# Moving forty-eight hand-over markers and output copies between VectorE, SyncE and ScalarE in a hand-ordered attention and MoE kernel

## The chip, the cores and the metric

The kernel runs on one core of one Trainium2 chip. The metric is device time in microseconds (us) for one launch. Before the change the median of three runs is 328.45 us (328.18 to 328.79).

The engines are TensorE (PE, its weight loads shown apart as PEld), VectorE (DVE), ScalarE (ACT), GpSimd (POOL) and SyncE (SP). Each has its own queue of instructions. Here SyncE computes nothing: it issues DMAs and carries markers that only wait and signal.

## The reference

Softcapped attention over 8 batches of 12 heads, 448 positions, 64 wide, followed by a block with two input matrices and an elementwise maximum:

```python
scores = cap * tanh(scale * q @ k.T / cap)
attn = exp(scores - max) / sum(exp(scores - max))
x = (attn @ v), heads joined to rows of 768
out = maximum(x @ w1, x @ w2) @ w_out      # 768 -> 1024 -> 768
```

## The kernel before, in words

**Tiling and stages.** The heads are taken in 48 pairs (`i`) and 24 quads of heads (`t`). Of a pair, `S i j` computes a block of scores on TensorE (L522), `T` and `E` run tanh and exp on ScalarE (L527, L544), `A` and `B` add up exponentials on VectorE (L556, L561), `VL` and `V` multiply by the values on TensorE (L608, L614), and `N` normalizes on VectorE into `xT` (L626, L629). From quad 5 on the queries and keys of a quad are turned by a DMA transpose that SyncE issues (`cr t`, line 483, `qkT<-kqs`). `qkT` has two buffers, so the transpose for quad `t` must wait until the last scores of quad `t-2` have read theirs.

The block behind the attention is rewritten as relu(x(w1-w2)) w_out + x(w2 w_out). It is cut into 120 groups, and each group accumulates in one PSUM bank: `stage1` groups make 128 columns of `gT` for one batch (448 columns stream per matmul, operands `xT` and `wd_sb`), `stage2` groups make 128 rows by 384 columns of output (operands `xT`, `wm_sb` for six steps, then `gT`, `wo_sb` for eight). Every two batches have 30 groups.

**Two half matmuls at a time.** A step of 128 contraction rows is split into two matmuls of 64 rows, one on each half of TensorE's rows. `M x y n` issues `n` times a first-half matmul of group `x` on the one row half and a second-half matmul of group `y` on the other (lines 640 to 656; all of these stand at L653 in the profile). A group does all its steps of one half, then all of the other half. While a group changes from one row half to the other, the first matmul of the new half must not start before the last one of the old half has left the PSUM bank.

**The hand-over.** `Group.hand_over(eng)` (line 660) writes a marker, an instruction that does nothing, into the queue of engine `eng` (L662). The marker waits for the group's last matmul of the old half; the group's first matmul of the new half waits for the marker (line 655). `H g` puts it on VectorE, `Hs g` on SyncE. An engine runs its queue in the order of the program, so a marker also waits for what stands ahead of it there, and holds up what stands behind it.

**The order.** The whole program is one string, `ORDER` (from line 10), executed literally under a manual schedule. No planner changes it. Apart from `S`, `M` and so on, SyncE's queue gets `cr` (transposes), `st b t` (two output stores each, L684, L685, L689) and the `Hs` markers. VectorE's queue gets the `H` markers between its sums, normalizations, the relu of stage 1 (L674) and `ev g`, which copies a finished stage-2 bank to the output buffer (L710). `eva g` does that copy on ScalarE (L708). POOL issues the loads.

Places that the later parts speak of, in the order string of before: `cr 11`, `H 29` and `H 28` (lines 78, 79 and 80), `cr 16`, `H 55` (line 119), `Hs 70` (line 146), `st 6 1` with `H 102`, and `st 6 2` with `H 105` (line 198).

Of the kernel before, what the change touches and what calls it, by code (L numbers as in the profile page):

```python
# [70 lines left out]
T 18 0; M 26 25 2; H 24; M 26 25 1; M 24 25 1; lk 23 1; M 24 25 1; E 17 0 2; H 26; M 24 25 1; S 18 2; M 24 25 1;  # L71
lq 23 0; M 24 25 4; S 18 1; O 27 3; M 27 25 1; eva 24; M 27 25 1; A 8 1 1; M 27 25 1; M 27 26 1; T 18 1;
M 27 26 2; ev 25; M 27 26 3; B 8 0; T 18 2; M 27 26 1; st 1 4; M 27 26 3; A 8 0 2; M 27 26 1; Hs 27; E 17 2 3;
O 28 1; M 28 26 2; B 8 1; L 9; st 0 2; VL 8; TL 9; V 8 0 0 2; A 8 1 2; V 8 1 0 2; E 18 0 3; Y 8 2; V 8 0 2 3;
V 8 1 2 3; Y1 8; lk 24 0; S 19 0; M 28 26 1; M 28 27 1; Y2 8; M 28 27 1; lv 10 0; Hs 26; st 1 3; M 28 27 1;
Y3 8; M 26 27 3; lv 10 1; M 26 27 1; N 8 0; M 26 27 2; T 19 0; lv 10 2; M 26 27 1; Hs 28; M 26 27 1; N 8 1;
O 29 2; M 29 27 2; lv 10 3; EL 9; M 29 27 1; M 29 28 1; S 19 1; M 29 28 1; lk 24 1; M 29 28 2; T 19 1; ev 26;
S 19 2; M 29 28 1; ev 27; M 29 28 1; lq 24 0; cr 11; M 29 28 1; T 19 2; M 29 28 1; A 9 0 1; S 20 0; M 29 28 2;
lk 25 0; M 29 28 1; E 19 0 2; A 9 0 2; O 30 3; M 30 28 1; S 20 1; M 30 28 1; H 29; lk 25 1; M 30 28 1;
M 30 29 2; H 28; st 1 5; M 30 29 1; lq 25 0; M 28 29 2; T 20 0; M 28 29 1; A 9 1 1; M 28 29 4; T 20 1; B 9 0;  # L80
Hs 30; M 28 29 1; S 20 2; O 31 0; M 31 29 1; B 9 1; M 31 29 1; eva 28; M 31 29 1; M 31 30 2; T 20 2; ev 29;
M 31 30 1; O 32 1; M 32 30 2; H 31; st 1 6; M 32 30 1; E 19 2 3; L 10; ev 30; VL 9; V 9 0 0 2; TL 10; A 9 1 2;
V 9 1 0 2; M 32 31 1; E 20 0 3; Y 9 3; V 9 0 2 3; V 9 1 2 3; lk 26 0; Y1 9; S 21 0; M 32 31 2; Y2 9; lv 11 0;
O 33 3; M 33 31 1; Y3 9; M 33 31 1; Hs 32; M 33 31 1; lv 11 1; M 33 32 2; N 9 0; T 21 0; M 33 32 1; O 34 2;
M 34 32 1; lv 11 2; M 34 32 1; Hs 33; ev 31; M 34 32 1; EL 10; lv 11 3; S 21 1; N 9 1; M 34 33 3; lk 26 1;
T 21 1; O 35 0; M 35 33 2; Hs 34; M 35 33 1; M 35 34 1; lq 26 0; ev 32; S 21 2; S 22 0; M 35 34 1; T 21 2;
ev 33; M 35 34 1; lk 27 0; O 36 1; M 36 34 2; A 10 0 1; Hs 35; M 36 34 1; E 21 0 2; M 36 35 1; lk 27 1; S 22 1;
ev 34; M 36 35 2; O 37 3; M 37 35 1; A 10 0 2; lq 27 0; M 37 35 1; Hs 36; M 37 35 1; M 37 36 1; T 22 0;
M 37 36 1; ev 35; M 37 36 1; O 38 2; M 38 36 2; A 10 1 1; Hs 37; cr 12; M 38 36 1; T 22 1; M 38 37 1; S 22 2;
B 10 0; M 38 37 2; T 22 2; O 39 0; M 39 37 1; ev 36; M 39 37 2; E 21 2 3; H 38; B 10 1; M 39 38 3; ev 37; L 11;  # L90
VL 10; TL 11; A 10 1 2; V 10 0 0 2; V 10 1 0 2; E 22 0 3; Y 10 1; V 10 0 2 3; V 10 1 2 3; Y1 10; S 23 0;
M 39 38 2; Y2 10; M 39 38 2; Y3 10; M 39 38 4; N 10 0; O 40 3; M 40 38 2; T 23 0; Hs 39; M 40 38 1; M 40 39 1;
N 10 1; M 40 39 1; Hs 38; M 40 39 1; EL 11; M 38 39 2; lk 28 0; S 23 1; M 38 39 3; T 23 1; A 11 0 1; lv 12 0;
S 23 2; M 38 39 2; cr 13; A 11 0 2; M 38 39 1; lv 12 1; T 23 2; O 41 1; M 41 39 1; S 24 0; ev 38; M 41 39 2;
lv 12 2; M 41 40 1; E 23 0 2; M 41 40 1; ev 39; S 24 1; M 41 40 1; lv 12 3; M 41 40 3; lk 28 1; M 41 40 1;
st 2 0; M 41 40 3; T 24 0; M 41 40 1; A 11 1 1; lq 28 0; O 42 2; M 42 40 3; H 41; T 24 1; B 11 0; M 42 41 1;
S 24 2; Hs 40; lk 29 0; M 42 41 2; B 11 1; M 40 41 1; T 24 2; M 40 41 1; lk 29 1; M 40 41 4; E 23 2 3;
M 40 41 1; lq 29 0; M 40 41 1; O 43 0; M 43 41 1; ev 40; L 12; VL 11; A 11 1 2; TL 12; V 11 0 0 2; V 11 1 0 2;
E 24 0 3; Y 11 3; V 11 0 2 3; V 11 1 2 3; Y1 11; S 25 0; M 43 41 2; Y2 11; M 43 42 2; Y3 11; M 43 42 4; N 11 0;
# [687 lines left out]
```

## Time and profile before

| what | value |
|---|---|
| median of 3 runs | 328.45 us |
| the profiled execution | 328.8 us |
| its span, first to last instruction | 327.0 us |
| granted TensorE clock | 0.997 |
| instructions in the span | 9770 |

A profile shows one execution. Its span is 1.8 us shorter than that execution's own time, which in turn lies 0.35 us above the median of the three runs. Groups of instructions are named by line, engine and tiles, `out<-in`. "SPq" and "DVEq" are instructions that only the engine's sequencer handles (markers, DMA issues); they do not count as busy time. A matmul's record (323 ns for 384 columns, 349 ns for 448) is longer than the distance at which matmuls of one row half follow each other, because they are pipelined, so the PE's busy share says little about small holes.

### The profile page before, as it was taken

What the parts mean: (1) busy time and instruction counts of PE and PEld (TensorE: products, weight loads), DVE (VectorE), ACT (ScalarE), POOL (GpSimd) and SP (SyncE); (2) the same over time, 40 slices, a digit from 0 to 9 for tenths busy, and PEclk for the clock granted to TensorE, in tenths of its full rate; (3) what the DMA queues carried; (4) which work ended last, traced back from release to release, by engine and by line L of the source; (5) the groups of instructions that cost most, each with busy time, mean ns of one, the idle gap of its engine ahead of it and who ended that gap; (6) DMA issues with size and microseconds to landing.
All of it is one profiled execution on the core that took longest, in us unless ns stands there. A gap on an engine that the chain in (4) does not pass through costs nothing.

```text
span 327.0 us, 9770 instructions
## 1 busy us (share of the span) xinstructions
PE 319.7 (98%) x4136; PEld 183.2 (56%) x4138; DVE 243.4 (74%) x427; ACT 278.3 (85%) x273; POOL 161.7 (49%) x237
## 2 busy tenths in 40 slices
PE   7999999999999999999999999999999999999994
PEld 3554545555755564565566555546466556557662
DVE  3346999988888588977887879858878779775321
ACT  5999999999999999999999999989999999920000
POOL 7457583669572885386467648358458211000000
PEclk9999999999999999999999999999999999999998
DMA  7999999899999999989998999899999953023033
GB/s 175 195 200 175 272 268 93 92 126 143 169 160 114 146 241 209 122 110 166 191 132 91 216 182 124 95 129 168 178 129 152 166 138 46 2 60 88 0 98 96
DMA packets 134507, 46.28 MB, mean 142 GB/s; under 512 B 112320, under 2 KB 129472, under 8 KB 134464
## 3 DMA queue, kind: packets, MB, share of 16 engines
q0 software_dynamic: 94592, 25.02, 76.7%
q1 hardware_dynamic: 39424, 19.99, 30.5%
q8 instruction: 32, 0.52, 0.7%
q10 hardware_dynamic: 448, 0.66, 0.6%
q14 instruction: 11, 0.09, 0.1%
HBM read 47.78 MB, written 11.01 MB: 180 GB/s over the span
## 4 chain that ended last, share of the span: by engine, by line
PE 93%; ACT 3%; DMA 1%; SPq 1%; DVE 0%; issue 0%
PE mm L653 61%; PE s L522 9%; PE s L614 9%; PE mm L439 5%; PE s L536 2%; ACT e L527 2%; PE mm L581 2%; PE s L608 2%; PE mm L648 1%; DMA kr<-in_k_dram 1%; PE mm L466 1%; ACT e L544 1%; PE mm L574 1%; PE mm L424 0%; SPq L689 0%; ACT kqs L316 0%
## 5 line engine op out<-in xcount | busy, mean ns | idle before, releaser
L527 ACT ACTIVATE e<-s 128x896 bf16<-128x896 f32 x144 | 125.9, 930 | 4.0 <-PE s L522 3.8
L544 ACT ACTIVATE e<-e 128x2688 bf16<-128x2688 bf16 (+2 forms) x72 | 123.0, 1712 | 0.1
L653 PE MATMUL mm<-wo_sb,gT 64*128 64x384 bf16 x864 | 115.0, 323 | 0.7 <-SPq L662 0.7
L653 PE MATMUL mm<-wm_sb,xT 64*128 64x384 bf16 x648 | 101.8, 323 | 0.0
L653 PE MATMUL mm<-xT,wd_sb 64*128 64x448 bf16 x768 | 97.8, 349 | 0.0
L336 POOL DMA_DIRECT2D kqs<-in_k_dram x76 | 54.6, 721 | 54.8 <-DMA qkT<-kqs 52.7
L653 PEld LDWEIGHTS <-gT 64*128 64x128 bf16 x864 | 58.0, 94 | 27.1 <-SPq L662 1.1
L653 PEld LDWEIGHTS <-wd_sb 64*128 64x128 bf16 x768 | 49.7, 94 | 26.1 <-issue 2.2
L653 PEld LDWEIGHTS <-xT 64*128 64x128 bf16 x648 | 49.7, 94 | 19.8 <-issue 1.3
L522 PE MATMUL s<-qkT 64*128 64x448 bf16 x288 | 52.4, 352 | 0.4 <-ACT e L527 0.4
L360 POOL DMA_DIRECT2D vp<-in_v_dram x48 | 30.4, 638 | 36.1 <-PE s L522 22.7
L674 DVE TENSOR_SCALAR gT<-mm 128x448 bf16<-128x448 f32 x64 | 38.9, 618 | 5.9 <-PE mm L653 4.8
L710 DVE COPY osb<-mm 128x384 f32<-128x384 f32 x49 | 26.2, 555 | 17.4 <-PE mm L653 16.6
L336 POOL DMA_DIRECT2D kqs<-in_q_dram x38 | 35.1, 923 | 4.6 <-issue 1.9
L614 PE MATMUL s<-e,vp 128*32 128x448 bf16 x576 | 35.5, 354 | 0.0
L556 DVE TENSOR_TENSOR esum<-e 128x896 bf16<-128x896 bf16 x42 | 25.8, 617 | 12.0 <-ACT e L544 11.7
L629 DVE TENSOR_TENSOR xT<-s,inv 64x448 bf16<-64x448 f32 x48 | 29.9, 622 | 0.9
L556 DVE TENSOR_TENSOR esum<-esum,e 128x896 bf16<-128x896 bf16 x42 | 26.0, 623 | 4.4 <-ACT e L544 3.2
L522 PEld LDWEIGHTS <-qkT 64*128 64x128 bf16 x288 | 18.2, 94 | 19.2 <-issue 10.9
L561 DVE TENSOR_TENSOR esum<-esum,el 64x896 bf16<-64x896 bf16 x42 | 26.0, 619 | 1.1
L586 DVE STREAM_TRANSPOSE st<-mm 128x448 f32<-128x448 f32 x24 | 15.6, 649 | 13.2 <-PE mm L581 12.2
L540 ACT ACTIVATE el<-s 128x896 bf16<-128x896 f32 x24 | 22.3, 928 | 2.4 <-PE s L536 1.9
(57 smaller groups left out, 249.7 us busy)
## 6 DMA issues: line engine op xcount, KB each, us to landing
out_dram<-osb SPq DMA_DIRECT2D x54, 192.0 KB, 4.4
vp<-in_v_dram POOLq DMA_DIRECT2D x38, 160.0 KB, 4.1
kqs<-in_q_dram POOLq DMA_DIRECT2D x46, 112.0 KB, 5.7
kqs<-in_k_dram POOLq DMA_DIRECT2D x76, 56.0 KB, 4.4
osb<-in_moe_w_dram POOLq DMA_DIRECT2D x4, 512.0 KB, 6.9
w2b<-in_moe_w_dram POOLq DMA_DIRECT2D x6, 256.0 KB, 6.6
wo_sb<-in_moe_w_out_dram POOLq DMA_DIRECT2D x4, 384.0 KB, 10.3
vp<-in_v_dram POOLq DMA_DIRECT2D x10, 128.0 KB, 7.7
```

The lines of the kernel that those rows point to most:

```text
L336: nc.gpsimd.dma_start(out=to, in_=x)
L360: nc.gpsimd.dma_start(out=to, in_=x)
L522: scored[i, j] = nc.tensor.matmul(s[:, h, :S], k_of(t, o, h, j), q_of(t, o, h)).ins
L527: nc.scalar.activation(expo[i][:, 2 * j : 2 * j + 2, :], slots[i, j][:, :, :S], AF.Tanh, scale=scale / cap)
L544: nc.scalar.activation(e, e, AF.Exp, scale=float(cap))
L556: nc.vector.tensor_add(d, e[:, 0:2, :] if j == 1 else d, e[:, 2 * j : 2 * j + 2, :])
L561: nc.vector.tensor_add(d, d, left_e[t][r, :, :])
L614: nc.tensor.matmul(vals[t][place(m, u), u, :S], w[:, m, :], expo[2 * t + o][:, 2 * j + h, :], start=False, stop=(j == NJ - 1))
L629: nc.vector.tensor_mul(x[64 - r : 128 - r], vals[t][r : r + 64, u, :S], sums[t, 3][64 - r : 128 - r])
L653: ins = nc.tensor.matmul(self.ps, w[r], x[r], start=first, stop=self.at == [self.n, self.n]).ins
L674: nc.vector.tensor_relu(gT[b // 2][:, f, cs], ps)
L710: nc.vector.tensor_copy(o[:, hs], ps)
```

## The change

Only `ORDER` differs: 48 of its 2405 entries name another engine, and none is moved, added or left out.

- 30 hand-overs go from VectorE to SyncE (`H` to `Hs`): of groups 26, 29, 28, 38, 44, 55, 54, 56, 58, 59, 58 again, 68, 74, 85, 84, 86, 88, 89, 100, 101, 102, 105, 109, 110, 111, 112, 115, 116, 117 and 116 again.
- 9 hand-overs go from SyncE to VectorE (`Hs` to `H`): of groups 40, 52, 53, 52 again, 61, 70, 83, 82 and 108.
- 8 output copies go from VectorE to ScalarE (`ev` to `eva`): of groups 102, 103, 112, 113, 114, 115, 116 and 117. One, of group 28, goes from ScalarE to VectorE.

The lines around the places named above, with only those entries that differ and their neighbours kept:

```diff
-cr 11; M 29 28 1; ... M 30 28 1; H 29; ... M 30 29 2; H 28; st 1 5; M 30 29 1;
+cr 11; M 29 28 1; ... M 30 28 1; Hs 29; ... M 30 29 2; Hs 28; st 1 5; M 30 29 1;
...
-Hs 37; cr 12; ... M 39 37 2; E 21 2 3; H 38; B 10 1; M 39 38 3;
+Hs 37; cr 12; ... M 39 37 2; E 21 2 3; Hs 38; B 10 1; M 39 38 3;
...
-cr 16; O 56 3; M 56 54 1; T 29 2; M 56 54 1; H 55; ... M 56 54 1; M 56 55 2; ... H 54;
+cr 16; O 56 3; M 56 54 1; T 29 2; M 56 54 1; Hs 55; ... M 56 54 1; M 56 55 2; ... Hs 54;
...
-cr 17; ... M 60 58 1; H 59; M 60 58 1; M 60 59 2; lq 37 0; H 58; st 3 5;
+cr 17; ... M 60 58 1; Hs 59; M 60 58 1; M 60 59 2; lq 37 0; Hs 58; st 3 5;
...
-cr 19; ... st 4 0; ... B 17 0; M 72 71 1; S 36 2; Hs 70; M 72 71 2; ... B 17 1; M 70 71 1;
+cr 19; ... st 4 0; ... B 17 0; M 72 71 1; S 36 2; H 70; M 72 71 2; ... B 17 1; M 70 71 1;
...
-cr 22; O 86 3; ... H 85; S 42 0; ... M 86 84 1; M 86 85 2; E 41 0 2; H 84;
+cr 22; O 86 3; ... Hs 85; S 42 0; ... M 86 84 1; M 86 85 2; E 41 0 2; Hs 84;
...
-Hs 103; st 6 1; M 104 102 1; M 104 103 2; H 102; M 104 103 1; M 102 103 3; Hs 104;
+Hs 103; st 6 1; M 104 102 1; M 104 103 2; Hs 102; M 104 103 1; M 102 103 3; Hs 104;
...
-M 105 103 2; ev 102; ... ev 103; ... M 106 104 2; st 6 2; H 105; M 106 104 1; M 106 105 2;
+M 105 103 2; eva 102; ... eva 103; ... M 106 104 2; st 6 2; Hs 105; M 106 104 1; M 106 105 2;
```

More of the change, by code (lines that the diff above doesn't have):

```diff
@@ L75 @@
[L75 to L99, printed above, removed]
@@ L205 @@
[L205 to L209 removed]
+T 18 0; M 26 25 2; H 24; M 26 25 1; M 24 25 1; lk 23 1; M 24 25 1; E 17 0 2; Hs 26; M 24 25 1; S 18 2;
@@ new lines @@
+N 8 1; O 29 2; M 29 27 2; lv 10 3; EL 9; M 29 27 1; M 29 28 1; S 19 1; M 29 28 1; lk 24 1; M 29 28 2; T 19 1;
+ev 26; S 19 2; M 29 28 1; ev 27; M 29 28 1; lq 24 0; cr 11; M 29 28 1; T 19 2; M 29 28 1; A 9 0 1; S 20 0;
+M 29 28 2; lk 25 0; M 29 28 1; E 19 0 2; A 9 0 2; O 30 3; M 30 28 1; S 20 1; M 30 28 1; Hs 29; lk 25 1;
+M 30 28 1; M 30 29 2; Hs 28; st 1 5; M 30 29 1; lq 25 0; M 28 29 2; T 20 0; M 28 29 1; A 9 1 1; M 28 29 4;
+T 20 1; B 9 0; Hs 30; M 28 29 1; S 20 2; O 31 0; M 31 29 1; B 9 1; M 31 29 1; ev 28; M 31 29 1; M 31 30 2;
@@ new lines @@
+T 20 2; ev 29; M 31 30 1; O 32 1; M 32 30 2; H 31; st 1 6; M 32 30 1; E 19 2 3; L 10; ev 30; VL 9; V 9 0 0 2;
+TL 10; A 9 1 2; V 9 1 0 2; M 32 31 1; E 20 0 3; Y 9 3; V 9 0 2 3; V 9 1 2 3; lk 26 0; Y1 9; S 21 0; M 32 31 2;
+Y2 9; lv 11 0; O 33 3; M 33 31 1; Y3 9; M 33 31 1; Hs 32; M 33 31 1; lv 11 1; M 33 32 2; N 9 0; T 21 0;
+M 33 32 1; O 34 2; M 34 32 1; lv 11 2; M 34 32 1; Hs 33; ev 31; M 34 32 1; EL 10; lv 11 3; S 21 1; N 9 1;
+M 34 33 3; lk 26 1; T 21 1; O 35 0; M 35 33 2; Hs 34; M 35 33 1; M 35 34 1; lq 26 0; ev 32; S 21 2; S 22 0;
@@ new lines @@
+M 35 34 1; T 21 2; ev 33; M 35 34 1; lk 27 0; O 36 1; M 36 34 2; A 10 0 1; Hs 35; M 36 34 1; E 21 0 2;
+M 36 35 1; lk 27 1; S 22 1; ev 34; M 36 35 2; O 37 3; M 37 35 1; A 10 0 2; lq 27 0; M 37 35 1; Hs 36; M 37 35 1;
+M 37 36 1; T 22 0; M 37 36 1; ev 35; M 37 36 1; O 38 2; M 38 36 2; A 10 1 1; Hs 37; cr 12; M 38 36 1; T 22 1;
+M 38 37 1; S 22 2; B 10 0; M 38 37 2; T 22 2; O 39 0; M 39 37 1; ev 36; M 39 37 2; E 21 2 3; Hs 38; B 10 1;
+M 39 38 3; ev 37; L 11; VL 10; TL 11; A 10 1 2; V 10 0 0 2; V 10 1 0 2; E 22 0 3; Y 10 1; V 10 0 2 3;
@@ new lines @@
+st 2 1; M 42 43 1; lv 13 1; T 25 2; M 42 43 1; S 26 0; A 12 0 2; M 42 43 2; lv 13 2; M 42 43 1; E 25 0 2; Hs 44;
+M 42 43 1; S 26 1; M 42 43 1; lv 13 3; O 45 1; M 45 43 2; ev 42; M 45 43 1; lk 30 1; M 45 44 2; ev 43;
+M 45 44 1; T 26 0; O 46 2; M 46 44 1; lq 30 0; A 12 1 1; M 46 44 1; Hs 45; cr 14; M 46 44 1; M 46 45 1; T 26 1;
+B 12 0; S 26 2; lk 31 0; M 46 45 2; O 47 0; M 47 45 1; ev 44; T 26 2; M 47 45 1; lk 31 1; M 47 45 1; H 46;
+B 12 1; M 47 46 1; E 25 2 3; M 47 46 1; lq 31 0; st 2 2; M 47 46 1; ev 45; O 48 3; M 48 46 1; L 13; VL 12;
@@ new lines @@
+A 12 1 2; TL 13; V 12 0 0 2; V 12 1 0 2; E 26 0 3; Y 12 1; V 12 0 2 3; V 12 1 2 3; Y1 12; S 27 0; lv 14 0;
+M 48 46 2; Y2 12; M 48 47 1; Y3 12; M 48 47 1; lv 14 1; M 48 47 1; O 49 1; M 49 47 2; Hs 48; ev 46; lv 14 2;
+M 49 47 1; T 27 0; M 49 48 2; N 12 0; lv 14 3; M 49 48 1; O 50 2; M 50 48 2; EL 13; Hs 49; ev 47; M 50 48 1;
+S 27 1; M 50 49 1; N 12 1; M 50 49 1; T 27 1; M 50 49 1; O 51 0; M 51 49 2; Hs 50; M 51 49 1; lk 32 0;
+M 51 50 2; ev 48; S 27 2; S 28 0; lk 32 1; M 51 50 1; ev 49; T 27 2; O 52 3; M 52 50 2; Hs 51; lq 32 0;
@@ new lines @@
+A 13 0 1; M 52 50 1; M 52 51 1; E 27 0 2; M 52 51 1; ev 50; S 28 1; M 52 51 1; lk 33 0; O 53 1; M 53 51 1;
+A 13 0 2; M 53 51 1; H 52; cr 15; M 53 51 1; M 53 52 1; lk 33 1; M 53 52 1; ev 51; M 53 52 1; T 28 0; M 53 52 2;
+A 13 1 1; M 53 52 1; lq 33 0; M 53 52 2; T 28 1; M 53 52 1; B 13 0; S 28 2; M 53 52 2; T 28 2; O 54 2;
+M 54 52 1; B 13 1; M 54 52 1; H 53; M 54 52 1; M 54 53 2; H 52; E 27 2 3; M 54 53 1; M 52 53 1; L 14; VL 13;
+TL 14; V 13 0 0 2; A 13 1 2; V 13 1 0 2; E 28 0 3; Y 13 0; V 13 0 2 3; V 13 1 2 3; Y1 13; S 29 0; M 52 53 2;
@@ new lines @@
+lk 36 1; M 59 58 3; T 31 1; ev 56; S 31 2; M 59 58 1; lq 36 0; M 59 58 1; ev 57; cr 17; M 59 58 1; T 31 2;
+M 59 58 1; S 32 0; A 15 0 1; M 59 58 1; lk 37 0; M 59 58 2; E 31 0 2; A 15 0 2; O 60 3; M 60 58 1; S 32 1;
+lk 37 1; M 60 58 1; Hs 59; M 60 58 1; M 60 59 2; lq 37 0; Hs 58; st 3 5; M 60 59 1; M 58 59 2; T 32 0;
+M 58 59 1; A 15 1 1; M 58 59 4; T 32 1; B 15 0; Hs 60; M 58 59 1; S 32 2; O 61 1; M 61 59 1; ev 58; M 61 59 1;
+T 32 2; M 61 59 1; M 61 60 1; B 15 1; M 61 60 2; E 31 2 3; O 62 2; M 62 60 1; ev 59; M 62 60 1; H 61; M 62 60 1;
@@ new lines @@
+M 66 64 1; lk 39 0; M 66 64 1; A 16 0 1; Hs 65; M 66 64 1; E 33 0 2; M 66 65 1; S 34 1; ev 64; lk 39 1;
+M 66 65 2; O 67 3; M 67 65 1; A 16 0 2; M 67 65 1; Hs 66; lq 39 0; M 67 65 1; M 67 66 1; T 34 0; M 67 66 1;
+ev 65; M 67 66 1; O 68 0; M 68 66 2; A 16 1 1; Hs 67; cr 18; M 68 66 1; T 34 1; M 68 67 1; S 34 2; B 16 0;
+M 68 67 2; T 34 2; O 69 1; M 69 67 1; ev 66; M 69 67 2; E 33 2 3; Hs 68; B 16 1; M 69 68 3; ev 67; L 17; VL 16;
+TL 17; A 16 1 2; V 16 0 0 2; V 16 1 0 2; E 34 0 3; Y 16 2; V 16 0 2 3; V 16 1 2 3; Y1 16; S 35 0; M 69 68 2;
@@ new lines @@
+M 89 88 3; E 43 0 2; A 21 0 2; O 90 3; M 90 88 1; S 44 1; M 90 88 1; Hs 89; M 90 88 1; M 90 89 2; Hs 88;
+M 90 89 1; st 5 5; M 88 89 2; T 44 0; M 88 89 1; A 21 1 1; M 88 89 4; T 44 1; B 21 0; M 88 89 1; Hs 90; S 44 2;
+O 91 2; M 91 89 1; ev 88; M 91 89 1; T 44 2; M 91 89 1; M 91 90 1; B 21 1; M 91 90 2; E 43 2 3; O 92 0;
+M 92 90 1; ev 89; M 92 90 2; L 22; st 5 6; ev 90; VL 21; TL 22; V 21 0 0 2; H 91; A 21 1 2; V 21 1 0 2;
+E 44 0 3; M 92 91 1; Y 21 1; V 21 0 2 3; V 21 1 2 3; Y1 21; S 45 0; lv 23 0; M 92 91 2; Y2 21; O 93 3;
@@ new lines @@
+M 93 91 1; Y3 21; M 93 91 1; lv 23 1; Hs 92; M 93 91 1; M 93 92 1; T 45 0; M 93 92 1; N 21 0; lv 23 2;
+M 93 92 1; O 94 1; M 94 92 2; Hs 93; ev 91; lv 23 3; EL 22; M 94 92 1; S 45 1; M 94 93 1; N 21 1; M 94 93 2;
+T 45 1; O 95 2; M 95 93 2; Hs 94; M 95 93 1; M 95 94 1; ev 92; S 45 2; S 46 0; M 95 94 1; T 45 2; ev 93;
+M 95 94 1; O 96 0; M 96 94 2; A 22 0 1; Hs 95; M 96 94 1; E 45 0 2; M 96 95 1; S 46 1; ev 94; M 96 95 2; O 97 3;
+M 97 95 1; A 22 0 2; M 97 95 1; Hs 96; M 97 95 1; M 97 96 1; T 46 0; M 97 96 1; ev 95; M 97 96 1; O 98 1;
@@ new lines @@
+S 47 2; M 98 99 2; O 101 0; M 101 99 1; A 23 0 2; T 47 2; M 101 99 2; M 101 100 1; ev 98; M 101 100 2; E 47 0 2;
+M 101 100 1; ev 99; M 101 100 4; st 6 0; M 101 100 3; O 102 1; M 102 100 2; E 47 2 3; Hs 101; M 102 100 1;
+A 23 1 1; M 102 101 2; Hs 100; M 102 101 1; B 23 0; VL 23; V 23 0 0 2; B 23 1; V 23 1 0 2; M 100 101 1;
+A 23 1 2; M 100 101 4; Y 23 2; V 23 0 2 3; V 23 1 2 3; Y1 23; M 100 101 3; Y2 23; O 103 2; M 103 101 2; Y3 23;
+eva 100; M 103 101 1; M 103 102 2; eva 101; M 103 102 1; N 23 0; M 103 102 4; N 23 1; M 103 102 4; O 104 3;
@@ L210 @@
+Hs 116; M 114 115 6; O 117 0; M 117 115 2; eva 114; M 117 115 1; M 117 116 2; eva 115; M 117 116 4; st 7 4;
+M 117 116 5; M -1 116 2; Hs 117; M -1 116 1; M -1 117 2; Hs 116; M -1 117 1; M 116 117 8; M -1 117 2; eva 116;
+M -1 117 1; O 118 1; M 118 118 1; eva 117; M 118 118 4; st 7 5; M 118 118 9; O 119 2; M 119 119 2; ev 118;
+M 119 119 12; ev 119; st 7 6;
 """
```

194 lines of the change are left out of this document (80 added, 114 removed).

## The prediction

> **What bounds the kernel now.** I read first the page's busy shares, the slices and the chain that ended last.
>
> ```profile
> PE 319.7 (98%) x4136; PEld 183.2 (56%) x4138; DVE 243.4 (74%) x427; ACT 278.3 (85%) x273; POOL 161.7 (49%) x237
> ...
> ACT  5999999999999999999999999989999999920000
> ...
> PE 93%; ACT 3%; DMA 1%; SPq 1%; DVE 0%; issue 0%
> ```
>
> TensorE (PE) is busy for 98% of the span and makes up 93% of the chain. ScalarE is full until near slice 35, and after that TensorE works alone for some 40 us. So only time that TensorE loses or wins counts. Next, the view of the waits, to see which of the two full engines waits for the other.
>
> ```profile
> ACT e L527 <- PE s L522: 3.8, 6, 0.8
> ...
> PE mm L653 <- SPq L662: 0.7, 1, 0.7
> PE s L522 <- ACT e L527: 0.4, 1, 0.4
> ```
>
> Between scores and tanh, ScalarE waits for TensorE (3.8 us), hardly the other way (0.4 us). So a delay of TensorE is not given back by ScalarE, beyond about 0.4 us. The middle row is the subject of the change: among 134 hand-overs, TensorE has waited visibly for one, a marker on SyncE. The view of line 662 gives their counts:
>
> ```profile
> L662 SPq EVENT_SEMAPHORE  x84: 17/17/17, 49.5 to 311.4; - x84
> L662 DVEq EVENT_SEMAPHORE  x50: 21/21/21, 64.7 to 316.0; - x50
> ```
>
> A marker itself takes 17 ns on SyncE and 21 ns on VectorE, so a change of engine costs or saves nothing by itself. What counts is what stands ahead of the marker in its queue. The timeline around the one wait (SyncE's rows, then TensorE's) shows hand-over 70:
>
> ```profile
> 212.31 3.57 SPq L483 DMA_TRANSPOSE qkT<-kqs  x1
> 215.99 1.17 SPq L689 DMA_DIRECT2D out_dram<-osb  x2
> 216.09 0.49 PE L653 MATMUL mm<-wm_sb,xT 64*128 64x384 bf16 x4
> 217.27 0.33 PE L653 MATMUL mm<-wo_sb,gT 64*128 64x384 bf16 x1 [0.69 <-SPq L662]
> 217.27 0.33 PE L653 MATMUL mm<-wm_sb,xT 64*128 64x384 bf16 x1
> ```
>
> SyncE was busy with a transpose until 215.88 and with two stores until 217.16. The marker came behind them, and TensorE went on at 217.27, which is **0.11 us after SyncE was free**. The four matmuls at 216.09 are two pairs, 0.16 us apart, so TensorE could have gone on at 216.41. It lost 0.86 us. Both row halves start at 217.27: the second-half matmul of group 71 did not run on while the one ahead of it waited for a marker.
>
> **The change part by part.** *Nine markers leave SyncE.* That of group 70 stops paying 0.86 us, if VectorE is not late there; the sums ahead of it in VectorE's queue start before TensorE needs it. The other eight stood at free places and stand at free places on VectorE; I take nothing, between 4 ns (21 against 17) and 0.56 us each (one VectorE operation such as the copies below, if the marker had to wait for its end), and stay at the low end because the view of the waits names no marker of the 50 on VectorE.
>
> *Thirty markers go to SyncE.* What stands ahead of them there? The view of the transposes' line and one more stretch of the timeline:
>
> ```profile
> L483 SPq DMA_TRANSPOSE qkT<-kqs x19: 1295/1636/3571, 54.8 to 259.8; - x19
> ```
>
> ```profile
> 119.32 1.29 SPq L483 DMA_TRANSPOSE qkT<-kqs  x1
> 120.72 1.18 SPq L689 DMA_DIRECT2D out_dram<-osb  x2
> ```
>
> ```profile
> L662 SPq EVENT_SEMAPHORE  x1: 17/17/17, 122.0 to 122.0; - x1
> ```
>
> A transpose holds SyncE for 1.30 us at the least, 1.64 in the median, 3.57 at the most. The store behind it starts at 120.72, after the transpose's end at 120.61, and the marker of group 30, behind the store's end at 121.90, comes at 122.0. So nothing passes. The order string then says which moved markers stand directly behind a transpose or a store with TensorE close behind: groups 29 (cr 11), 38 (cr 12), 55 (cr 16), 59 (cr 17), 85 (cr 22), 102 (st 6 1) and 105 (st 6 2). On VectorE they passed freely. These are SyncE's rows for them, one narrow window of the timeline each (that of cr 11 is above):
>
> ```profile
> 133.89 1.64 SPq L483 DMA_TRANSPOSE qkT<-kqs  x1
> 177.02 2.03 SPq L483 DMA_TRANSPOSE qkT<-kqs  x1
> 188.51 1.87 SPq L483 DMA_TRANSPOSE qkT<-kqs  x1
> 248.22 1.59 SPq L483 DMA_TRANSPOSE qkT<-kqs  x1
> 292.92 1.11 SPq L689 DMA_DIRECT2D out_dram<-osb  x2
> 296.38 1.11 SPq L689 DMA_DIRECT2D out_dram<-osb  x2
> ```
>
> And these are the rows of TensorE in which the first matmul behind the hand-over starts, in the same order with group 29 first:
>
> ```profile
> 119.98 0.32 PE L653 MATMUL mm<-wm_sb,xT 64*128 64x384 bf16 x1
> 135.24 0.32 PE L653 MATMUL mm<-wm_sb,xT 64*128 64x384 bf16 x1
> 177.83 0.66 PE L653 MATMUL mm<-wm_sb,xT 64*128 64x384 bf16 x6
> 190.32 0.32 PE L653 MATMUL mm<-wm_sb,xT 64*128 64x384 bf16 x1
> 249.02 0.66 PE L653 MATMUL mm<-wm_sb,xT 64*128 64x384 bf16 x6
> 293.72 0.32 PE L653 MATMUL mm<-wo_sb,gT 64*128 64x384 bf16 x1
> 296.11 1.15 PE L653 MATMUL mm<-xT,wd_sb 64*128 64x448 bf16 x10
> ```
>
> The last row starts with group 106's first step; its matmuls come in pairs 0.19 us apart, and group 105 changes halves with the fourth pair, at 296.68. The new start of each is SyncE's start plus duration plus 0.11, and the wait is that less the old start:
>
> - 29: 119.32+1.29+0.11 = 120.72, less 119.98: **0.74**
> - 38: 133.89+1.64+0.11 = 135.64, less 135.24: **0.40**
> - 55: 177.02+2.03+0.11 = 179.16, less 177.83: **1.33**
> - 59: 188.51+1.87+0.11 = 190.49, less 190.32: **0.17**
> - 85: 248.22+1.59+0.11 = 249.92, less 249.02: **0.90**
> - 102: 292.92+1.11+0.11 = 294.14, less 293.72: **0.42**
> - 105: 296.38+1.11+0.11 = 297.60, less 296.68: 0.92. This store waits for copies 102 and 103, which move to ScalarE:
>
> ```profile
> 295.22 1.13 DVE L710 COPY osb<-mm 128x384 f32<-128x384 f32 x2 [2.04 <-PE mm L653]
> ```
>
> ```profile
> L708 ACT COPY osb<-mm x5: 479/480/518, 105.3 to 291.0; 128x384 f32<-128x384 f32 x5
> ```
>
> Two copies at 0.48 take 0.96 instead of 1.13, the store starts 0.17 earlier: **0.75**.
>
> The sum is 4.71 us. It is an upper account, since the matmul of the other row half that stands ahead of the waiting one still runs: the half that sets the pace may lose one matmul (0.16 to 0.19, I take 0.2) less at each place but 102, where the waiting matmul stands first. That gives 0.54+0.20+1.13+0+0.70+0.42+0.55 = 3.54. I take the middle, 4.1.
>
> The wait at 55 can't be dodged by an earlier transpose. cr 16 writes the buffer that scores S 29 2 read, and starts as these end:
>
> ```profile
> 176.64 0.35 PE L522 MATMUL s<-qkT 64*128 64x448 bf16 x2
> ```
>
> 176.64+0.35 is 176.99, the transpose starts at 177.02. It and the hand-over are tied to TensorE's own progress, 0.81 us apart, while the shortest transpose and the 0.11 take 1.41.
>
> The other moved markers have the cover to hide theirs: 26, 44, 56, 58 (first), 74, 86, 88, 100 and 116 (first) change halves with other groups' pairs between, 109 to 112 have SyncE to themselves, and 115 to 117 follow stores that end before their matmul does; with the cover gone each would cost what its transpose or store still takes, 1.1 us at most for a store. Groups 54, 28 and 58 (second) follow the late markers above and find their matmul done. Groups 68, 89 and 101 stand behind a transpose or store that ends about as TensorE arrives; I count nothing, and up to 0.3 each in the range. A store that now waits behind a marker (st 1 5, st 3 3, st 5 3) starts up to one such wait later; four output buffers cover it, and if they didn't, a copy and a bank would be late by the same wait. The **copies** in the tail run on an idle ScalarE at 0.48 against 0.56; they gate no matmul before and gain nothing. Copy 28 adds one VectorE copy of 0.56 ahead of copy 29, whose bank isn't due.
>
> Sum: +4.1 − 0.86 − 0.2 (between nothing and the 0.4 that TensorE waits for ScalarE I take the middle) = **+3.1 us** (3.04, rounded up for the uncounted three). The profiled execution took 328.8 with a span of 327.0; I expect a span of 330.1 there and 331.9 in all. That execution lies 0.35 above the median of the runs, so the forecast is 328.45 + 3.1 = **331.6**.
>
> One rule bears on this sum. The Trainium skill, TensorE: Matmul & The Clock Gate, The mechanism, says that matmuls start and end strictly in queue order. The trace differs where a row half is merely busy:
>
> ```profile
> 120.47 0.32 PE L653 MATMUL mm<-wm_sb,xT 64*128 64x384 bf16 x1
> 120.62 0.32 PE L653 MATMUL mm<-wo_sb,gT 64*128 64x384 bf16 x1
> ```
>
> The second row is group 28's step, which stands ahead of group 29's in the order, yet starts 0.15 later. By the rule no half runs on, the full 4.71 count, and the time is 328.45 + 4.71 − 0.86 − 0.2 = 332.1 (a rival, below).
>
> **The rivals.** *A, faster: SyncE passes a marker soon after a transpose begins.* Then cr 11, 16 and 22 cost nothing, only group 70's 0.86 remains: 327.6. It decides if the marker behind cr 16 passes within 177.83−177.02−0.11 = 0.70 us. For it: none of the rows above has a marker directly behind a transpose. Against it: a store there started only after the transpose's end (120.72 after 120.61), and the shortest record is 1.30. Chance 0.05.
>
> *B, part of it is absorbed.* Transposes are at their shortest (1.30: groups 29, 55 and 85 lose 0.74, 0.60 and 0.61, less 0.2 each; 38 and 59 nothing; 102 and 105 0.42 and 0.55) and TensorE's waits for ScalarE vanish: 0.54+0.40+0.41+0.97−0.86−0.4 = +1.1, 329.5. With half of that, 330.4. Against it: the 0.40 that ScalarE's wait measures is all there is to absorb. Chance 0.15.
>
> *C, longer transposes.* One of the five is as long as the longest, which adds 1.5 if it is cr 16 (3.57 − 2.03), or the uncounted 68, 89 and 101 pay 0.3 each: 4.71 − 0.86 + 1.5 = +5.4, 333.8. For it: the loads that TensorE paces shift, and durations run to 3.57. Chance 0.15.
>
> *D, the strict order above*: 332.1, chance 0.12. *E, the queues don't change as the string says* (a marker bound elsewhere): 328.4, chance 0.03. The forecast, between +2.3 and +3.6, has 0.50.
>
> **How the numbers follow.** About 0.2%, or 0.66 us, is what a measurement of this kernel can tell from no change. Faster: A, 0.05, and 0.01 of E. Same: the rest of E and a corner of B, 0.04. Slower: 0.90. The range goes from B's end, 329.5, to C's, 333.8; it leaves out A, E and longer tails.
>
> **What would show it.** In the changed profile, the view of waits should show TensorE's matmuls at L653 waiting for SPq L662 several times, longest near group 55's 1.3 us, at about 120, 178, 250, 294 and 298 us, each 0.11 us behind the end of a SyncE transpose or store; hand-over 70's 0.69 should be gone. ScalarE's waits for TensorE should grow. If TensorE passes 178 us without a hole, A holds; if holes are there and the span isn't longer, B does.

## The result, and the profile after

The changed kernel takes **332.68 us** in the median of four runs (332.07 to 333.33), the kernel before 328.31 beside it (328.01 to 328.79): a ratio of 1.0132, 95% interval 1.0105 to 1.0159, or 4.4 us. The forecast was 331.6 in a range of 329.5 to 333.8. The profiled execution, the shortest of the four, took 332.07 with a span of 330.3, which is 3.3 us above the span of before. One execution further down, the profiled one of the second series with four markers moved, took 336.13 us at a granted clock of 0.995, and only the distances around its hand-overs are used.

Busy shares and the end of ScalarE's slices, from the page of the changed kernel:

```profile
PE 322.0 (98%) x4138; PEld 185.2 (56%) x4138; DVE 239.9 (73%) x420; ACT 282.1 (85%) x280; POOL 161.7 (49%) x237
...
ACT  4999999999999998999999899999999999911120
...
PE 91%; ACT 3%; DMA 2%; SPq 1%; DVE 1%; issue 0%
```

TensorE still sets the end: 98% busy, and most of the chain. Eight copies went to ScalarE and one to VectorE, so ScalarE has 280 instructions instead of 273 and VectorE 420 instead of 427. The view of the waits (engine and line, what it waited for: total us, times, longest):

```profile
ACT e L528 <- PE s L523: 5.8, 9, 1.3
...
PEld L654 <- SPq L663: 4.0, 6, 0.9
...
PE mm L654 <- SPq L663: 1.7, 4, 0.5
...
PE s L523 <- ACT e L528: 0.4, 1, 0.4
```

In before one weight load and one matmul waited for SyncE's marker, both at hand-over 70. Now it is six weight loads and four matmuls; a hole in which both waited stands in both rows. ScalarE waits 5.8 us for TensorE instead of 3.8; TensorE's own 0.4 us of waiting for ScalarE hasn't gone. The view of the marker's line confirms the move, and that a marker's own time stays 17 and 21 ns:

```profile
L663 SPq EVENT_SEMAPHORE  x105: 17/17/17, 49.9 to 319.2; - x105
L663 DVEq EVENT_SEMAPHORE  x29: 21/21/21, 65.0 to 302.6; - x29
```

Lines of the changed kernel are one higher than before's; in the kernels of the experiments, but for the kernel before once more, they are about ten lower (matmuls at L643, markers at L652, transposes at L473).

Now the timeline around hand-over 55 (SyncE's transpose 16, then TensorE):

```profile
177.97 1.55 SPq L484 DMA_TRANSPOSE qkT<-kqs  x1
...
178.77 0.32 PE L654 MATMUL mm<-wm_sb,xT 64*128 64x384 bf16 x1
179.62 0.27 PEld L654 LDWEIGHTS <-xT 64*128 64x128 bf16 x5 [0.92 <-SPq L663]
179.62 0.66 PE L654 MATMUL mm<-wm_sb,xT 64*128 64x384 bf16 x5 [0.53 <-SPq L663]
```

The transpose ends at 177.97+1.55 = 179.52, and TensorE goes on at 179.62. In between, no matmul starts on either row half. At 85 the picture is the same, and at 102 and 105 pairs of stores stand where the transpose stood (SyncE's rows from narrow windows):

```profile
249.15 1.50 SPq L484 DMA_TRANSPOSE qkT<-kqs  x1
...
250.77 0.27 PEld L654 LDWEIGHTS <-xT 64*128 64x128 bf16 x5 [0.88 <-SPq L663]
...
294.68 1.11 SPq L690 DMA_DIRECT2D out_dram<-osb  x2
...
295.90 0.33 PE L654 MATMUL mm<-wo_sb,gT 64*128 64x384 bf16 x1 [0.24 <-SPq L663]
...
298.49 1.10 SPq L690 DMA_DIRECT2D out_dram<-osb  x2
...
299.70 0.36 PE L654 MATMUL mm<-xT,wd_sb 64*128 64x448 bf16 x2 [0.44 <-SPq L663]
```

At all four places TensorE goes on 0.10 to 0.12 us behind the end of SyncE's row. The number in brackets on a matmul is less than what is lost, because it begins where the modelled end of the matmul before lies. A better measure is **the distance between the same two matmuls in two traces**, since over most stretches without an edit it repeats to 0.02 us. For hand-over 55: these are the last scores ahead of transpose 16 and the last scores of the next pair, first in before, then in the changed kernel.

```profile
176.64 0.35 PE L522 MATMUL s<-qkT 64*128 64x448 bf16 x2
180.78 0.36 PE L522 MATMUL s<-qkT 64*128 64x448 bf16 x2
```

```profile
177.58 0.35 PE L523 MATMUL s<-qkT 64*128 64x448 bf16 x2
182.43 0.51 PE L523 MATMUL s<-qkT 64*128 64x448 bf16 x2
```

4.14 us have become 4.85, a loss of 0.71. Worked out in this way over the whole kernel, against a second trace of before (span 326.1, below), the time went here:

| stretch (what lies in it) | before again | changed | changed again |
|---|---|---|---|
| start of the span to scores 3 0 | 19.05 | 19.51 | 19.07 |
| scores 10 0 to 19 2 (waits for transposed data) | 56.82 | 57.13 | 56.82 |
| to scores 20 2 (hand-over 29) | 3.99 | 3.99 | **6.32** |
| to group 33 (copy 28) | 5.06 | 5.33 | 4.94 |
| scores 29 2 to 30 2, to 31 2 (55) | 4.14, 7.34 | 4.85, 7.49 | 4.89, 7.48 |
| to 32 2, to 36 2 (59) | 3.99, 23.79 | 4.12, 23.67 | 4.13, 23.65 |
| to 37 0 (hand-over 70) | 4.01 | 4.01 | 4.01 |
| scores 41 2 to 42 2, to 43 2 (85) | 4.14, 7.39 | 4.81, 7.48 | 5.23, 7.48 |
| scores 47 2 to group 104 (101) | 9.42 | 9.50 | 9.49 |
| to group 105 (102) | 2.44 | 2.85 | 2.85 |
| to group 107 (105) | 2.08 | 2.89 | 2.88 |
| to 112, to 117, to 119 | 5.86, 10.07, 7.42 | 5.67, 10.28, 7.64 | 5.68, 10.28, 7.64 |

Everything between these stretches is equal to 0.02. In the changed kernel's trace, copy 28 costs 0.27, hand-over 55 0.86 with the 0.15 behind it, 85 0.76, 101 0.08, 102 0.41, 105 0.81, and the end 0.24; 59's 0.13 is given back in the next stretch. That is **3.4 us** tied to the order. Another 0.8 us lies in the first two rows. None of it is behind an entry that differs: the first of these, `H 26`, comes after scores 15 2, and what the second row is longer by lies ahead of them (scores 10 0 to 15 2 took 34.76 instead of 34.45).

### The profile page after: what moved, and what is told of

Its sections match the earlier page's. It is cut to its first block, busy times and chain, and to the rows that moved or that the text cites. A ratio compares the mean times of both kernels' runs of the same rounds, so it can differ in the third digit from the quotient of the medians.

```text
span 330.3 us, 9775 instructions
## 1 busy us (share of the span) xinstructions
PE 322.0 (98%) x4138; PEld 185.2 (56%) x4138; DVE 239.9 (73%) x420; ACT 282.1 (85%) x280; POOL 161.7 (49%) x237
## 4 chain that ended last, share of the span: by engine, by line
PE 91%; ACT 3%; DMA 2%; SPq 1%; DVE 1%; issue 0%
PE mm L654 58%; PE s L523 9%; PE s L615 9%; PE mm L440 5%; DMA qkT<-kqs 2%; ACT e L528 2%; PE s L537 2%; PE s L609 2%; PE mm L467 2%; PE mm L582 1%; PE mm L649 1%; PE mm L480 1%; ACT e L545 1%; SPq L690 1%; PE mm L575 1%; PE mm L425 0%
## 5 line engine op out<-in xcount | busy, mean ns | idle before, releaser
L654 PE MATMUL mm<-wo_sb,gT 64*128 64x384 bf16 x864 | 117.3, 323 | 0.2 <-SPq L663 0.2
L654 PE MATMUL mm<-wm_sb,xT 64*128 64x384 bf16 x648 | 104.4, 323 | 1.0 <-SPq L663 1.0
L654 PEld LDWEIGHTS <-gT 64*128 64x128 bf16 x864 | 59.8, 94 | 24.8 <-issue 0.7
L654 PEld LDWEIGHTS <-wd_sb 64*128 64x128 bf16 x768 | 48.7, 94 | 28.3 <-issue 2.6
L654 PEld LDWEIGHTS <-xT 64*128 64x128 bf16 x648 | 50.5, 94 | 21.3 <-SPq L663 2.5
L709 ACT COPY osb<-mm 128x384 f32<-128x384 f32 x12 | 5.8, 481 | 28.5 <-PE mm L654 28.2
L711 DVE COPY osb<-mm 128x384 f32<-128x384 f32 x42 | 22.6, 555 | 4.9 <-PE mm L654 3.9
```

The source lines that it names most:

```text
L654: ins = nc.tensor.matmul(self.ps, w[r], x[r], start=first, stop=self.at == [self.n, self.n]).ins
L711: nc.vector.tensor_copy(o[:, hs], ps)
```

## The experiments

Two theories stood against each other. **Queue theory**: a marker costs what SyncE still has ahead of it in its queue, a transpose or stores. **Marker price**: a hand-over on SyncE, or by another engine, costs something wherever it stands. Edits are those of the order string; "us" is the median of the runs, the interval that of the ratio to before.

**The changed kernel once more**, for a second trace (the third column above).

> The changed kernel once more, nothing edited, for a second profile and more times. In the first profile of it TensorE lost 0.84 us at hand-over 55, 0.80 at 85, 0.79 at 105, 0.41 at 102, 0.15 at 38, 0.13 at 59 and 0.45 where group 32 waits for output copy 28, won 0.85 at hand-over 70, and lost nothing at hand-over 29, since transpose 11 had ended early. Its four times lie in two pairs, 332.1 to 332.2 and 333.1 to 333.3. Queue theory: the same holes at the same places, and the upper pair comes from transposes that end later relative to TensorE, at hand-over 29 (0.74 forecast) above all. Rival, a price of each marker on SyncE: no holes stand out, the delay grows evenly over the thirty places.

Measured: 332.99 us (332.11 to 333.66), ratio 1.0137 (1.0117 to 1.0157); span 331.9. The holes at 55, 85, 102 and 105 are there again, and one at 29 that the first trace didn't have. The timeline there, in the first trace and in this one:

```profile
118.85 1.38 SPq L484 DMA_TRANSPOSE qkT<-kqs  x1
```

```profile
119.18 0.92 POOL L326 DMA_DIRECT2D kqs<-in_q_dram  x1
...
120.93 1.30 SPq L473 DMA_TRANSPOSE qkT<-kqs  x1
121.06 0.71 POOL L326 DMA_DIRECT2D kqs<-in_k_dram  x1 [0.96 <-DMA kqs<-in_q_dram]
...
122.33 0.09 PEld L643 LDWEIGHTS <-xT 64*128 64x128 bf16 x1 [2.45 <-SPq L652]
```

The transpose reads what POOL's loads bring. In that stretch the view of SyncE's waits has only these two rows:

```profile
SPq L473 <- DMA kqs<-in_k_dram: 2.7, 1, 2.7
SPq L473 <- DMA kqs<-in_q_dram: 2.0, 1, 2.0
```

In the first trace the same view has TensorE in their place:

```profile
SPq L484 <- PE mm L654: 3.1, 1, 3.1
```

So transpose 11 started 2.08 us later than in the first trace, although TensorE was 0.75 us earlier there (the first two rows of the table), because a load landed late, and the marker behind it, which TensorE needed, came that much later: a loss of 2.33 us.

**Ten markers back on VectorE.**

```diff
-Hs 29; ... Hs 28; ... Hs 38; ... Hs 55; ... Hs 54; ... Hs 59; ... Hs 85; ... Hs 84; ... Hs 102; ... Hs 105;
+H 29; ... H 28; ... H 38; ... H 55; ... H 54; ... H 59; ... H 85; ... H 84; ... H 102; ... H 105;
```

> The changed kernel with ten of the thirty moved hand-overs back on VectorE: those of groups 29, 28, 38, 55, 54, 59, 85, 84, 102 and 105, all that stand directly behind a SyncE transpose or store with TensorE close behind. Twenty stay on SyncE. Queue theory: the waits there go, what is left is minus 0.85 us (hand-over 70) plus 0.45 (copy 28): 327.9 us, ratio to before 0.999. Rival, a price of each marker on SyncE: two thirds of the 4.4 us stay, 331.2 us, ratio 1.009.

Measured: 329.0 us (11 runs, one of them 656.36 us, twice the others, for a reason that the record doesn't show), ratio 1.0015 (1.0004 to 1.0025). That is above the 327.9 expected, which counted on 0.85 us at hand-over 70 (below). Twenty of the thirty moved markers remain on SyncE, and the 4.4 us are gone but for some 0.5, of which its trace puts 0.27 at copy 28 and 0.08 at 101. Around hand-over 55 the timeline has a still longer transpose, and the view of the markers' line shows VectorE's two passing while it runs:

```profile
178.31 1.94 SPq L473 DMA_TRANSPOSE qkT<-kqs  x1
```

```profile
L652 DVEq EVENT_SEMAPHORE  x2: 21/21/21, 178.6 to 179.3; - x2
```

The distance of scores 29 2 to 30 2 is 4.14 again. These are the markers that paid, and the queue is what they paid for, not the number of markers on SyncE.

**Ten back, and copy 28 back on ScalarE too.**

```diff
-ev 28;
+eva 28;
```

> The changed kernel with the ten hand-overs behind transposes and stores back on VectorE and copy 28 back on ScalarE. The ten alone came to 329.0 us (ratio 1.0015). Bank theory for copy 28: 0.45 us less, 328.55 us, ratio 1.000; less than that by what hand-over 70's hole is worth in a usual run, at most 0.85 us: 327.7 us, ratio 0.9975. Rival, copy 28's 0.45 us is given back later (the one-entry kernel's time rose by 0.0005, interval -0.0019 to 0.0029): it stays at 329.0 us.

Measured: 329.18 us (12 runs), ratio 1.0025 (1.0007 to 1.0043). The 328.55 expected was missed, and no gain over ten back can be told from the runs. In its trace the stretch to group 33 is back at 5.06, as it should be; but the stretch from scores 10 0 to 15 2, ahead of every edit, took 0.79 longer there than in before's. Against such accidents 0.27 us is too little for the medians.

**Copy 28 alone**, in the kernel before.

```diff
-eva 28;
+ev 28;
```

> The kernel before with one entry changed: output copy 28 on VectorE instead of ScalarE. First profile of the changed kernel: group 32, which takes the bank of group 28, starts 0.05 us behind the end of that copy, 0.45 us late. Bank theory: the same here, 328.75 us, ratio 1.0014, and group 32's first matmul directly behind the VectorE copy. Rival, the delay there comes from hand-over 31, which stands behind two copies on VectorE: then group 31 starts its second half late and group 32 does not wait for the copy. My prediction's own reading: nothing, 328.3 us.

Measured: 328.66 us (12 runs), ratio 1.0005 (0.9981 to 1.0029), span 327.2. The stretch to group 33 takes 5.33 instead of 5.06, as in the changed kernel. Why can be seen in the changed kernel's timeline, in one narrow window for the copy and one for the first matmul of group 32:

```profile
123.57 0.56 DVE L711 COPY osb<-mm 128x384 f32<-128x384 f32 x1
...
124.18 0.37 PE L654 MATMUL mm<-xT,wd_sb 64*128 64x448 bf16 x2
```

The copy ends at 124.13, and the group that takes over its bank starts 0.05 later. In the trace of this experiment the two stand at 123.38 and 123.44, and three more traces with copy 28 on VectorE have the same 0.05. So TensorE does wait for this copy, and the rival falls. The 0.45 expected was the delay of group 32's first matmul; at group 33 the trace shows 0.27 us, which the runs can't resolve.

**Hand-over 70 alone**, in the kernel before.

```diff
-Hs 70;
+H 70;
```

> The kernel before with one entry changed: hand-over 70 on VectorE instead of SyncE. Queue theory: the 0.86 us that TensorE lost behind a transpose and two stores goes, and nothing else changes: 327.45 us, ratio 0.9974; ScalarE's idle time of 1.08 us before the scores that follow shrinks by the same. Rival, ScalarE or VectorE takes over as the bound behind it: TensorE waits for ScalarE's tanh or VectorE's sums within the next 15 us and the time stays at 328.3 us.

Measured: 328.57 us (11 runs), ratio 1.0008 (0.9994 to 1.0021). No gain, where 0.86 had been read from the trace. In its own trace the stretch to scores 37 0 is 4.01, without a hole, and no later stretch is longer than in before, so the rival, a bound that takes over behind it, isn't there either.

**The kernel before again**, to see why.

```diff
 (no edit)
```

> The kernel before once more, for a second trace. If the 3.57 us of transpose 19 was the accident of one execution, the hole at hand-over 70 is 0.1 to 0.6 us here instead of 0.86; if it belongs to the order of this kernel, it is 0.8 to 0.9 again. Time 328.2 to 328.8 by both.

Measured: 328.41 us (12 runs); the profiled execution took 327.83 with a span of 326.1, and its view of the waits has no row with SyncE's marker. Transpose 19, ahead of hand-over 70:

```profile
212.22 1.62 SPq L483 DMA_TRANSPOSE qkT<-kqs  x1
```

It takes 1.62 us instead of 3.57, starting at the same place. In the five traces with `Hs 70` on SyncE in its old place (without that of 336.13 us), the stretch to scores 37 0 lost 0.87, 0.52, 0.18, 0 and 0 us, a mean of 0.3. So the hole comes in some executions, and its size of 0.86 was that of **one execution**.

**Hand-over 29 back**, in the changed kernel.

```diff
-Hs 29; ... Hs 28;
+H 29; ... H 28;
```

> The changed kernel with only the hand-overs 29 and 28 that stand behind transpose 11 back on VectorE. In three profiles so far transpose 11 ended early in one of the changed kernel (hole at hand-over 29: none) and at 122.23 us in another (hole: 2.44 us); its start is set by a load that POOL issues, not by TensorE. Queue theory: the hole at 29 is gone for good, the times lose their upper part: median 331.6 to 332.2 us instead of 332.7 to 333.0, ratio 1.010 to 1.011, holes at 38, 55, 59, 85, 102 and 105 unchanged. Rival, the upper runs come from the start of the kernel (its first scores were 0.1 us early to 0.7 us late between profiles): spread and median stay, ratio 1.013.

Measured: 332.26 us (332.17 to 332.75), ratio 1.0131 (1.0116 to 1.0146). The 331.6 to 332.2 expected was missed by little, and the ratio is the rival's: the median hardly moves. The spread shrinks from 332.07 to 333.66 (both series of the changed kernel) to 332.17 to 332.75. That fits a hole at 29 that comes in some executions, but with four runs it isn't more than a hint.

**Four markers alone**, in the kernel before.

```diff
-H 55; ... H 54; ... H 85; ... H 84;
+Hs 55; ... Hs 54; ... Hs 85; ... Hs 84;
```

> The kernel before with four entries changed: hand-overs 55, 54, 85 and 84 on SyncE, all behind transposes 16 and 22. Queue theory: holes of 0.85 us at 55 and 0.8 to 1.2 us at 85, none at 54 and 84: 330.2 to 330.6 us, ratio 1.0050 to 1.0065. Rival, a price of each marker (4.4 us over thirty): 4 times 0.15, 329.1 us, ratio 1.002. My prediction's own sizes, 0.7 to 0.9 and 1.13 to 1.33: 330.4 to 330.7 us.

Measured: 331.39 us (330.29 to 331.94), ratio 1.0094 (1.0078 to 1.0111). The holes are in its trace, 0.92 and 0.77 with 0.14 and 0.09 behind them, 1.92 in all. The median, above the 330.2 to 330.6 expected, says 3.2. Of the rest, this trace has 1.0 us between scores 10 0 and 15 2 and 0.8 ahead of scores 3 0, where nothing is edited. Therefore it went once more:

> The kernel before with only 55, 54, 85 and 84 on SyncE, once more, since its first trace held 1.9 us of holes at 55 and 85 and the runs lay 3.2 us above before. If the rest was an execution that happened to wait elsewhere: holes of 0.7 to 1.1 us at 55 and at 85 again, nothing else, 330.0 to 330.7. If transposes 16 and 22 are often longer than in the traces so far (1.50 to 2.57 us): up to 1 us more at either hand-over, 330.7 to 332.2, and the holes of this trace show it.

Measured: 331.37 us (11 runs), ratio 1.0081 (1.0055 to 1.0108). Its profiled execution took 336.13 us; the intervals at its two hand-overs are 5.13 and 5.13 instead of 4.14, with 0.15 and 0.10 behind them, 2.23 in all. The timeline at 55:

```profile
182.99 1.83 SPq L473 DMA_TRANSPOSE qkT<-kqs  x1
184.92 0.27 PEld L643 LDWEIGHTS <-xT 64*128 64x128 bf16 x5 [1.20 <-SPq L652]
```

Longer transposes do make longer holes, the second expectation, but they don't fill the whole of it. In this series the fastest runs differ by 330.58 − 327.86 = 2.7 and the medians by 3.0; what fills the 0.8 between 2.2 and 3.0 stays open.

This trace shows one thing more. Transpose 11, which waited for loads, started only at 124.39, and the marker of group 30, behind it and a pair of stores, passed at 127.1: the stretch to group 33 took 9.34 us instead of 5.06. `Hs 30` stands on SyncE in the kernel before too, so before isn't free of such a hole when a load is late.

**Stores alone**, in the kernel before.

```diff
-H 102; ... H 105;
+Hs 102; ... Hs 105;
```

> The kernel before, with the hand-overs of 102 and 105 on SyncE, behind st 6 1 and st 6 2, and nothing else changed. Queue theory: holes of 0.4 us at 102 and 0.8 us at 105 (a store pair issues in 1.1 us), and up to 0.4 us more at the end, where the halves of groups 112 to 119 keep an offset: span 1.2 to 1.6 us above that of before, 329.4 to 330.1. Rival, that the stores hold nobody and the tail loses time by the copies on ScalarE: no hole, the time of before, 328.2 to 328.7.

Measured: 329.92 us (329.55 to 330.08), ratio 1.0044 (1.0032 to 1.0056), 1.4 us; span 328.1. The holes are 0.41 and 0.89, and the stretches to 112, 117 and 119 change by −0.18, +0.21 and +0.22, although nothing is edited there and the copies stand on VectorE. So the end's loss belongs to these two hand-overs, not to the copies. Matmul by matmul against before, counted from group 104, the second row half is 1.35 us late directly behind hand-over 105 and 1.54 in group 110, the first one only 1.12 at the start of group 112; in group 118, where each matmul takes both halves, it is 1.54.

**Markers ahead of what held them.** All thirty markers stay on SyncE; the transposes and stores move behind them.

```diff
-cr 16; O 56 3; ... Hs 55; ... Hs 54;
+O 56 3; ... Hs 55; ... Hs 54; cr 16;
...
-Hs 103; st 6 1; ... Hs 102;
+Hs 103; ... Hs 102; st 6 1;
```

The same was done with cr 11, 12, 17, 18 and 22 and with st 6 2.

> The changed kernel with all thirty markers still on SyncE, but transposes 11, 12, 16, 17, 18 and 22 and the stores 6 1 and 6 2 put behind the markers that they stood ahead of (a few matmuls later in the order). Queue theory: it is the place in the queue and not the engine, so the holes at 29, 38, 55, 59, 85, 102 and 105 go; copy 28's 0.45 us stays: 328.7 to 329.2 us, ratio 1.001 to 1.002. Rival, a marker on SyncE costs by itself: 332.5 us, ratio 1.012. If the later transposes make scores or loads late, TensorE waits for transposes at L512 or so instead, and the time lies between.

Measured: 331.2 us (329.6 to 332.21), ratio 1.0087 (1.0065 to 1.0109). The holes at 29, 38, 55, 59, 85, 102 and 105 are gone, as queue theory says, but the time isn't back to the 328.7 to 329.2 expected. The waits and the timeline name two new places, 30 and 60, of which this is the second (SyncE up to the marker, which passed at 195.8):

```profile
191.75 1.52 SPq L473 DMA_TRANSPOSE qkT<-kqs  x1
193.38 2.38 SPq L679 DMA_DIRECT2D out_dram<-osb  x2
195.86 0.87 PEld L643 LDWEIGHTS <-wd_sb 64*128 64x128 bf16 x11 [2.11 <-SPq L652]
```

Transposes 11 and 17 had moved behind the markers of 28 and 58, and so had come, with the stores, directly ahead of those of 30 and 60, which had always been on SyncE. The stretch from scores 32 2 to 36 2 lost 2.03 us: the same price, paid by another marker. The second version leaves transposes 11 and 17 where they were, with the four markers 29, 28, 59 and 58 on VectorE.

> The changed kernel, with 26 of its 30 moved markers still on SyncE (those of 29, 28 second, 59 and 58 second are back on VectorE, so that transposes 11 and 17 stay where they were), and with transposes 12, 16, 18 and 22 and the stores st 6 1 and st 6 2 moved behind the markers of 38, 54, 68, 84, 102 and 105. Queue theory: a marker costs only what stands ahead of it on SyncE, so no hole at 29, 38, 55, 59, 85, 102 or 105, and none at 30 or 60, where the first order of this kind had 0.8 and 2.2 us: within 0.3% of before, 328.2 to 329.4. Rival, that a hand-over on SyncE costs by itself wherever it stands: 26 of 30 markers stay there, so at least two thirds of the loss stays, 331 to 333.

Measured: 329.18 us (12 runs), ratio 1.0018 (1.0003 to 1.0034). Of SyncE's markers its waits show little:

```profile
PEld L643 <- SPq L652: 0.6, 2, 0.4
```

Twenty-six of the thirty markers on SyncE, and it costs about 0.7 us, of which its trace puts 0.27 at copy 28 and 0.33 at hand-over 56, whose marker now stands behind transpose 16. Marker price would have kept two thirds of the loss, so it falls. No version here beats the kernel before.

## Why the prediction was right, point by point

- **What bounds the kernel: right.** TensorE's holes came out as time, and ScalarE gave nothing back; its waits grew by 2.0 us.
- **Hand-overs 55, 85, 102, 105: right mechanism and place.** Forecast in the upper account 1.33, 0.90, 0.42 and 0.75, measured 0.86, 0.76, 0.41 and 0.81. 55 was mis-sized by its transpose, 2.03 us in the trace of before and 1.55 in this one. The formula holds with the transpose of the run: start plus duration plus 0.11, less 0.81 behind the start, gives 0.85, 1.06 and 1.13 for 1.55, 1.76 and 1.83 us, and the three traces (changed, four markers alone, and these again) lost 0.86, 1.06 and 1.14. Two more traces with the marker on SyncE, of transposes of 1.59 and 1.58 us, lost 0.89 both times. The shorter transpose doesn't look like the luck of one trace: in these five it took 1.55 to 1.83 us, in seven traces with hand-over 55 on VectorE 1.74 to 2.57. Why is not shown.
- **"The half that sets the pace may lose one matmul less": failed.** The losses at 55 are the full upper amount, and no matmul starts between 178.77 and 179.62 on either half. Up to the next scores the half with one matmul ahead did lose less, 0.71 against 0.85 on the other half, but the 0.15 came due in the next stretch. The Trainium skill, TensorE: Matmul & The Clock Gate, The mechanism, says that matmuls start in queue order. The trace agrees where a matmul waits for a marker (this hole), and disagrees where a row half is merely busy (120.62 ahead of 120.47 in the order, quoted in the prediction). Rival D counted the holes rightly.
- **The −0.86 for hand-over 70: failed.** It was read from one execution, with the longest transpose of its trace, 3.57 us. Over five traces it is worth 0.3, and the runs of that edit alone show no gain.
- **Hand-over 29 at 0.74: mis-sized.** It is 0 in one trace and 2.33 in the other, because transpose 11 waited for TensorE in the one and for a late load in the other. In the trace of before, too, it had waited for a load (3.0 us), and the prediction took its start there as fixed. 38 and 59 came to nothing once the next stretch was counted (0.57 forecast).
- **Copy 28: failed.** The prediction looked at the bank of copy 29, which isn't due, and not at that of copy 28 itself: group 32 takes it over and starts 0.05 us behind the copy's end, which costs 0.27 us. The tail's 0.24 was not forecast either: it is what the row halves lost unequally at 102 and 105. 101 was 0.08, within the 0.3 allowed.
- **The −0.2 absorbed by ScalarE's waits: not seen.** The 0.4 stands in both.
- **The rivals.** A falls: no marker passes a transpose that has begun. B falls: the holes are time. E falls by the markers' counts. Of C, the transposes at 55 and 85 were shorter in the first trace, not longer, and 68, 89 and 101 came to 0.08; but hand-over 29 lost 2.33 in the second trace by a late start, where C had counted on long transposes.

So the mechanism and the places were right, and that the sum came as near as it did is partly luck, since errors balanced. Taken one by one, the forecast had +4.1 in holes and −1.1 in credits; the trace has 3.4, the credits are not there, and hand-over 29 adds to that in some executions. The holes that are tied to the order are shown by doing and undoing them. The remaining 0.5 to 1 us of the medians (4.4 against 3.4) is not placed: a late load at 29, longer transposes and the first stretches, which vary by over a microsecond without any edit, are each seen, but not in which shares. A late load at 29 can't be all of it: the four markers alone, with 29 on VectorE, already lie 0.8 to 1.3 above the holes of their traces, while ten back and the stores alone agree with theirs within 0.2.

On where SyncE's hold ends: the Trainium skill, Perfetto Trace Analysis, DMA Instruction — HWDGE (DVE, Sync), states that the recorded end of such a DMA is where the sequencer is free for its next instruction. The rows agree: the marker behind the transpose at 55 let TensorE go 0.10 us behind the recorded end.

## What to carry to other kernels

Before a marker, or any instruction that only waits and signals, goes to another engine, read what stands ahead of it in that queue, at that place: a transpose issued from the same queue held it for up to 3.6 us, a pair of stores for 1.1, at one place 2.4. If such an issue is moved away, look at the next marker in that queue, for it inherits the wait. And price a hole from several traces, and ask what starts the instruction that makes it: one that hangs on TensorE's own progress is late each time, one that hangs on a load or on its own length only sometimes.

## What the runs showed that was not expected

- The duration of the same transpose varies from one execution to the next without any edit near it: number 19 took 3.57, 3.23 and 1.62 us, number 16 from 2.03 to 2.57. Where a marker stands behind it, SyncE is held for all of it.
- Between such accidents TensorE's timing repeats to 0.01 us over stretches of 20 to 40 us, far finer than the medians tell. But one pair of traces can deceive: scores 42 2 to 43 2 took 7.34, 7.39 and 7.41 us in kernels without any edit near it. A small difference counts when it returns in each trace with the edit, as 101's 0.08 does in all seven.
- A hole can leave a trace behind itself: after 102 and 105, the stretches to groups 112, 117 and 119 took 0.19 less, 0.21 and 0.22 more, with nothing waiting in them for SyncE.
